# Window attention and SiLU MLP on one core: the second MLP product in float16 parts one group earlier, with w_out's two float32 parts joined on GpSimd

## The chip, the cores and the metric

One core of a Trainium2 chip. The metric is the device time of one execution in microseconds (us), the median of several runs. TensorE (PE) multiplies, VectorE (DVE), ScalarE (ACT) and GpSimd (POOL) work on tiles of 128 partitions, and SyncE (SP) issues most transfers. Each engine takes its own instructions in order and waits on semaphores for the others.

## The reference

```python
scores = scale * q @ k.T            # 8 batches x 8 heads x 576 rows, head size 64
scores = where((rel >= 0) & (rel < 128), scores + slope[h] * -abs(rel), -1e9)
x = softmax(scores) @ v             # joined to 4608 tokens x 512
h = x @ w_in                        # 512 x 2048
out = (h * sigmoid(h)) @ w_out      # 2048 x 512
```

All inputs and the output are float32.

## The kernel before

The 4608 tokens are taken in 9 groups of 512. A group g has 16 blocks f of 128 columns of the hidden layer, and the block n = 16 g + f is the unit of the MLP: `gemm1(n)` (L710) makes the 128 x 512 block of h, `act1` takes the tanh on ACT (L753), `act2` on DVE makes the activation from it and from h in PSUM (L762), `act3` writes its high part gh (L779), `act4` the rest gl (L796), and `gemm2(n)` (L917) adds gh and gl times w_out's block to four PSUM banks, with twelve matmuls of 128 x 512: (gh, high), (gh, low), (gl, high) for each of four token tiles.

Float32 accuracy comes from products of parts. In the early groups the parts are in the reduced float32 format fp32r: each weight block is held as a high and a low fp32r tile (`w_parts`, L983; the tags `w0_f` for w_in and `w1_f` for w_out). In later groups they are in float16, scaled by a power of two that a maximum over the weights gives. `IN16 = 2` and `OUT16 = 3` (L57) are the first groups whose first and second product use float16 parts. In groups below `OUT16`, act3 is a copy to fp32r and act4 runs on POOL (on DVE in the blocks at a group's edge, L807); from `OUT16` on, act3 is an ACT activation and act4 a `scalar_tensor_tensor` on DVE (L805).

The float16 weights are made in the middle of the kernel from the fp32r parts:

- `w_stat` (L237), 32 ACT activations, gives sums of squares; `wscale_finish` (L314) reduces them with a transpose, small DVE operations and a matmul to the two scales.
- For each of the 16 blocks of each matrix, `conv1` (L1009, ACT) writes the float16 high part, `conv2` (L1020, DVE) the remainder of the high part in float32, and `conv3` (L1028, DVE) adds the low part to it: three instructions, two of them on DVE.

The order of the work is written out by hand. The program runs through numbered steps; a step is half a `gemm1` or half a `gemm2`, so that a group is 64 steps: group 1 is steps 64 to 127, group 2 is 128 to 191. `put(step, function, ...)` files further work, which is issued ahead of the step's matmuls, by rank within a step (L1168: `normalize` first, then the activations, then `row_max` and `p_lo`, then all else). A step number fixes only where an instruction stands in its engine's queue; when it runs is decided by its waits.

The attention runs as such further work, one pair p (half a token tile's heads) in 8 steps: `scores` at step n (PE), `row_max` n + 1 (DVE), `exps` n + 2 and n + 3, `p_hi` (ACT) and `p_lo` (DVE) n + 3 to n + 5, a DMA transpose, `attend` n + 13 in the groups spoken of here (n + 12 from the third batch pair on), `normalize` (DVE) one step behind that. In group 2 the scores stand at steps 130, 138, 146, 154 and so on. PSUM's two banks with the tag `a` serve both the scores and the `attend` results, so `scores` of a pair must wait until `normalize`, two steps earlier, has read the bank. Every second pair, `load_v` (SP) fetches a tile rv, and `v_hi` (POOL, L427) and `v_lo` (DVE, L433) split it. In group 2 DVE also takes maxima of v for the next batches (`vscale_reduce`, L210).

In the kernel before, `STATS = 66` puts one `w_stat` in each step from 66 on, `CONV_IN = 106` starts w_in's conversions (four steps for each block, and three steps later from block 5 on: `CLEAR = 3`), and `CONV_OUT = 172` starts w_out's.

Of the kernel before, what the change touches and what calls it, by code (L numbers as in the profile page):

```python
# [6 lines left out]
F32 = mybir.dt.float32  # L7
# [26 lines left out]
NF = DFF // P  # L34
# [19 lines left out]
SLICE = 4  # L54


IN16, OUT16 = 2, 3  # L57
QK16 = 2
STATS16 = ("w1_10", "w1_11")
OWN = ("w1_12", "w1_13")  # L60
# [9 lines left out]
SUMS, SUMS_STEP = 332, 14  # L70
SUM_TAGS = tuple(f"w1_{k}" for k in range(7, 15))
MORE_TAGS = (("w1_15", 1), ("k", KSLOTS), ("k", KSLOTS))
STATS, CONV_IN, CONV_OUT = 66, 106, 172
CLEAR = 3
STEP = 8
LEAD = 14
XD = GT
# [20 lines left out]
def tile_window_attention_then_silu_mlp(ctx, tc, qk, qk16, v, w_in, w_out, distance, out):  # L98
    nc = tc.nc

    const = ctx.enter_context(tc.tile_pool(name="const", bufs=1))
    pool = ctx.enter_context(tc.tile_pool(name="pool", bufs=2))
    psum = ctx.enter_context(tc.tile_pool(name="psum", bufs=1, space=PSUM))

    ident = const.tile([P, P], F32, name="ident")
    tab = const.tile([P, H, 2 * P], BF16, name="tab")
    ones = const.tile([P, P], F32, name="ones")
# [32 lines left out]
    def f32(ap):  # L140
        return ap.bitcast(F32)
# [33 lines left out]
    vred = {}  # L175
# [59 lines left out]
    wsc = {}  # L235

    def w_stat(which, f):  # L237

        if f == 0:
            vred["w", which] = {"m": pool.tile([P, NF], F32, tag=f"stat{which}", bufs=1, name=f"stat{which}")}  # L240
        junk = pool.tile([P, DM], BF16, tag="xs", bufs=2, name=f"wj{which}_{f}")
        nc.scalar.activation(
            junk, f32(w_parts(f, which)[0]), AF.Square, accum_out=vred["w", which]["m"][:, f : f + 1]
        )
# [66 lines left out]
        flat = tab.rearrange("p h c -> p (h c)")  # L311
        nc.vector.tensor_scalar_mul(flat, flat, ratio)

    def wscale_finish(stage):  # L314

        if stage == 0:
            vred["w", "col"] = col = pool.tile([P, 3], F32, tag="vcol", name="vcolw")
            for k in range(2):
                nc.vector.tensor_reduce(col[:, k : k + 1], vred["w", k]["m"], axis=AX.X, op=ALU.max)
        elif stage == 1:  # L320
            ps = ps_of(next_tag("misc"), "vtw")
            for k in range(2):
                nc.tensor.transpose(ps[:1, k * P : (k + 1) * P], vred["w", "col"][:, k : k + 1], ident)
            vred["w", "row"] = row = pool.tile([P, 9], F32, tag="row", bufs=1, name="roww")
            c, inv = row[:1, 0:2], row[:1, 2:4]
            ci = c.bitcast(I32)
            nc.vector.tensor_reduce(c, ps[:1, : 2 * P].rearrange("p (k i) -> p k i", k=2), axis=AX.X, op=ALU.max)
            nc.vector.tensor_single_scalar(ci, ci, 0x7F800000, op=ALU.bitwise_and)
            nc.vector.tensor_single_scalar(ci, ci, 1, op=ALU.logical_shift_right)
            nc.vector.tensor_single_scalar(ci, ci, 0x1FC00000, op=ALU.add)  # L330
            nc.vector.tensor_single_scalar(ci, ci, 0x7F800000, op=ALU.bitwise_and)
            nc.vector.tensor_single_scalar(ci[:, 1:2], ci[:, 1:2], 1 << 23, op=ALU.add)
            nc.vector.tensor_single_scalar(inv.bitcast(I32), ci, -(14 << 23), op=ALU.add)
            nc.vector.tensor_scalar(ci, ci, -1, 268 << 23, op0=ALU.mult, op1=ALU.add)
        else:
            ps = ps_of(next_tag("misc"), "vsw")
            nc.tensor.matmul(ps[:, 0:4], ones[:1, :], vred["w", "row"][:1, 0:4], start=True, stop=True)
            t = pool.tile([P, 4], F32, tag="wsc", bufs=1, name="vscw")
            nc.vector.tensor_copy(t, ps[:, 0:4])
            for k in range(2):  # L340
                wsc["w", k] = t.rearrange("p (s k) -> p k s", k=2)[:, k]
# [641 lines left out]
    def w_parts(f, which):  # L983
        if which == 0:
            return [weight(kind, f).rearrange("p a b -> p (a b)") for kind in ("wih", "wil")]
        return weight("woh", f), weight("wol", f)
# [7 lines left out]
        minus(nc.gpsimd, lo, wraw.pop((f, which))[1], f32(hi))  # L994


    w16, rest = {}, {}

    def w16_tile(which, f):

        j, k = divmod(f, 2)
        if ("pair", which, j) not in w16:
            tag = f"w0_{NF // 2 + j if which else j}"
            w16["pair", which, j] = pool.tile([P, 2, 2, DM], F16, tag=tag, bufs=1, name=f"w16_{which}_{j}")
        t = w16["pair", which, j][:, k]
        w16[which, f] = t if which else t.rearrange("p a (c f) -> p a c f", c=NCC)
        return t

    def conv1(which, f):  # L1009
        hi = w_parts(f, which)[0]  # L1010
        if which or f:
            t = w16_tile(which, f)
            parts = [t[:, k] for k in range(2)]
        else:
            parts = [pool.tile([P, DM], F16, tag="xs", bufs=2, name=f"wi16_{k}_{f}") for k in range(2)]
        rest[which, f] = parts
        out16 = parts[0]
        nc.scalar.activation(out16, f32(hi), AF.Copy, scale=wsc["w", which][:, 0:1])

    def conv2(which, f):  # L1020
        hi, out16 = w_parts(f, which)[0], rest[which, f][0]
        r = pool.tile([P, DM], F32, tag="io", name=f"wr16_{which}_{f}")
        rest[which, f].append(r)
        nc.vector.scalar_tensor_tensor(
            out=r, in0=f32(hi), scalar=wsc["w", which][:, 0:1], in1=out16, op0=ALU.mult, op1=ALU.subtract
        )

    def conv3(which, f):  # L1028
        out16, low16, r = rest.pop((which, f))
        nc.vector.scalar_tensor_tensor(  # L1030
            out=low16, in0=f32(w_parts(f, which)[1]), scalar=wsc["w", which][:, 0:1], in1=r, op0=ALU.mult, op1=ALU.add
        )
        if not which and not f:

            t = w16_tile(0, 0)
            for k, part in enumerate((out16, low16)):
                nc.scalar.copy(t[:, k], part)
# [8 lines left out]
    def put(point, fn, *a):  # L1046
        plan.setdefault(max(point, at(0)), []).append((fn, a))

    for p in range(NPAIR):
        i, q = divmod(p, 2)  # L1050
        n = at(p)
# [48 lines left out]
        if q == 0:  # L1100
# [74 lines left out]
    with tc.manual_schedule():  # L1175
# [41 lines left out]
        for g in range(NG):  # L1217
# [3 lines left out]
            for f in range(NF):  # L1221
                n = g * NF + f
# [5 lines left out]
                while len(waiting) > left:  # L1228
                    k = waiting.pop(0)
# [70 lines left out]
```

## Time and profile before

| | |
|---|---|
| runs | 923.24, 923.34, 923.34 us; median 923.34 |
| the profiled execution | 923.45 us, of which its span (first to last instruction) is 921.7 |
| PE busy | 910.2 us (99%) |
| DVE busy | 697.8 us (76%) |
| ACT busy | 579.0 us (63%) |
| POOL busy | 204.2 us (22%) |
| mean granted TensorE clock | 0.999 |

All times of the trace are in us from the span's start. Group 2's matmuls run from 256.57 to about 362. PE is busy nearly all the time, so that the kernel's time is PE's own work plus the few places where PE waits; what the other engines do costs time only where PE, in its order, comes to an instruction whose operand is not there yet.

### The profile page before, as it was taken

How to read it: one execution, taken by the hardware profiler on the slowest of the kernel's cores; microseconds unless marked ns; L12 is line 12 of the kernel's file. 1: busy time of each engine (PE TensorE's matmuls, PEld its weight loads, DVE VectorE, ACT ScalarE, POOL GpSimd, SP SyncE). 2: the span in 40 equal slices, each digit the busy share in tenths (PEclk: the TensorE clock that was granted, in tenths of full speed). 3: DMA queues.
4: the chain of work that ended last, by engine and by line, in shares of the span. 5: the costliest groups of instructions: out<-in, count | busy, mean ns of one | idle time of the engine just before them, and what ended most of it. 6: DMA issues, size and time to landing. Idle time of an engine off the chain costs nothing.

```text
span 921.7 us, 17985 instructions
## 1 busy us (share of the span) xinstructions
PE 910.2 (99%) x6765; PEld 604.6 (66%) x6765; DVE 697.8 (76%) x1703; ACT 579.0 (63%) x1195; POOL 204.2 (22%) x195
## 2 busy tenths in 40 slices
PE   9999999999999999999999999999999999999998
PEld 7867777777787887555555555555555555557887
DVE  6889876446777778898778879888888876645675
ACT  7778887685556764666677756666766665533332
POOL 2343442222221221000000003455655300000000
PEclk9999999999999999999999999999999999999999
DMA  8977825243376655434698746444554454311000
GB/s 314 393 181 221 258 58 138 69 92 69 81 208 159 172 127 127 104 102 102 126 246 217 204 104 160 115 104 103 160 109 109 102 166 104 89 35 59 1 24 23
DMA packets 198182, 122.94 MB, mean 133 GB/s; under 512 B 166480, under 2 KB 167632, under 8 KB 198096
## 3 DMA queue, kind: packets, MB, share of 16 engines
q1 hardware_dynamic: 197664, 121.41, 50.2%
q8 instruction: 53, 0.87, 0.4%
q10 hardware_dynamic: 432, 0.39, 0.1%
q14 instruction: 33, 0.27, 0.1%
HBM read 71.96 MB, written 9.44 MB: 88 GB/s over the span
## 4 chain that ended last, share of the span: by engine, by line
PE 83%; DVE 6%; ACT 2%; issue 1%; DVEq 0%; ACTq 0%
PE o L933 33%; PE h L733 24%; PE h L738 8%; PE av L555 4%; PE h L705 4%; PE m L840 3%; PE sp L451 3%; PE sp L458 2%; DVE hr L505 1%; DVE gt L764 1%; DVE t L481 0%; ACT t L491 0%; DVE w L1030 0%; DVE vmx L210 0%; DVE x L148 0%
## 5 line engine op out<-in xcount | busy, mean ns | idle before, releaser
L933 PE MATMUL o<-w,gh 128*128 128x512 f16 (+1 forms) x1024 | 313.3, 387 | 0.3 <-ACT gh L791 0.3
L733 PE MATMUL h<-xt,w 128*128 128x512 f16 (+1 forms) x1344 | 266.7, 349 | 0.0
L933 PE MATMUL o<-w,gl 128*128 128x512 f16 (+1 forms) x512 | 197.3, 385 | 0.3 <-DVE gl L148 0.2
L733 PEld LDWEIGHTS <-w 128*128 128x128 f16 x1344 | 125.8, 98 | 103.1 <-issue 2.2
L760 ACT ACTIVATE gt<-h,gsc 128x512 f32<-128x512 f32 x112 | 76.8, 686 | 183.5 <-PE h L733 164.3
L764 DVE SCALAR_TENSOR_TENSOR gt<-gt,h 128x512 f32<-128x512 f32 x144 | 98.3, 683 | 87.7 <-ACT gt L760 87.0
L491 ACT ACTIVATE t<-t,mx 128x256 f32<-128x256 f32 (+1 forms) x288 | 125.8, 486 | 5.7 <-DVE mx L481 5.5
L505 DVE SCALAR_TENSOR_TENSOR hr<-t,hr 128x512 f16<-128x512 f32 (+1 forms) x128 | 96.7, 761 | 30.7 <-ACT hr L500 30.6
L933 PEld LDWEIGHTS <-gh 128*128 128x128 f16 x640 | 62.2, 98 | 74.2 <-ACT gh L793 0.3
L738 PE MATMUL h<-xh,w 128*128 128x512 f32 x256 | 89.8, 405 | 0.0
L427 POOL TENSOR_SCALAR v<-rv,vsc 128x512 f16<-128x512 f32 x30 | 28.0, 933 | 277.1 <-DMA rv<-v 177.5
L805 DVE SCALAR_TENSOR_TENSOR gl<-gt,gh 128x512 f16<-128x512 f32 x80 | 61.9, 774 | 33.8 <-ACT gh L793 32.7
L933 PEld LDWEIGHTS o<-w,gh 128*128 128x128 f32 x384 | 69.8, 188 | 15.9 <-ACT gh L791 0.8
L146 POOL TENSOR_TENSOR gl<-gt,gh 128x512 fp32r<-128x512 f32 x30 | 38.5, 1284 | 164.2 <-ACT gh L791 148.9
L500 ACT ACTIVATE hr<-t 128x512 f16<-128x512 f32 (+1 forms) x128 | 71.7, 595 | 2.0 <-DVE vmx L210 2.0
L793 ACT ACTIVATE gh<-gt 128x512 f16<-128x512 f32 x80 | 50.3, 629 | 26.0 <-DVE gt L764 23.3
L555 PEld LDWEIGHTS <-hl 128*128 128x128 f16 x1464 | 51.4, 98 | 16.5 <-issue 5.2
L481 DVE CUSTOM_DVE_ANT_0 t<-sp,tab,vsc 128x256 f32<-128x256 f32 (+1 forms) x144 | 58.4, 460 | 1.1 <-PE sp L451 0.7
L933 PEld LDWEIGHTS <-gl 128*128 128x128 f16 x320 | 31.3, 98 | 38.6 <-DVE gl L805 1.0
L146 POOL TENSOR_TENSOR w<-wm,w 128x512 fp32r<-128x512 f32 x32 | 43.4, 1355 | 59.3 <-ACT w L990 59.0
L555 PE MATMUL av<-v,hl 128*128 128x65 f16 (+1 forms) x1464 | 54.8, 193 | 1.6 <-DVE mx L481 1.6
L738 PEld LDWEIGHTS h<-xh,w 128*128 128x128 f32 x256 | 48.1, 188 | 12.3 <-issue 0.2
(183 smaller groups left out, 1357.2 us busy)
## 6 DMA issues: line engine op xcount, KB each, us to landing
r<-qk SPq DMA_DIRECT2D x36, 512.0 KB, 4.1
qs<-qk SPq DMA_DIRECT2D x18, 512.0 KB, 5.2
wr<-w_in SPq DMA_DIRECT2D x16, 512.0 KB, 6.6
wr<-w_out SPq DMA_DIRECT2D x16, 512.0 KB, 6.3
out<-ot SPq DMA_DIRECT2D x32, 256.0 KB, 2.5
rv<-v SPq DMA_DIRECT2D x30, 256.0 KB, 4.0
vm<-v SPq DMA_DIRECT2D x27, 256.0 KB, 5.6
q<-qk SPq DMA_DIRECT2D x18, 256.0 KB, 3.6
```

What stands on the lines that cost most here:

```text
L146: engine.tensor_sub(out, a, b)
L481: nc.vector.tensor_tensor_reduce(out=st[p]["t"][u][:, h, 2 * P - n :], in0=st[p]["sp"][h][:, u, o].rearrange("p o c -> p (o c)"), in1=tab[ ...
L491: nc.scalar.activation(x, x, AF.Exp, bias=st[p]["mx"][:, 2 * u + h : 2 * u + h + 1], scale=-1.0)
L500: nc.scalar.activation(split_of(p, u, hr)[:, 0], t[:, :, 2 * P - n :], AF.Copy, scale=PSCALE)
L505: nc.vector.scalar_tensor_tensor(out=hr[:, 1], in0=t[:, :, 2 * P - n :], scalar=PSCALE, in1=hr[:, 0], op0=ALU.mult, op1=ALU.subtract)
L555: nc.tensor.matmul(av[:, 2 * u + h, : rhs.shape[-1]], lhs, rhs, start=(n == 0), stop=(n == len(seq) - 1), skip_group_check=True,)
L733: nc.tensor.matmul(o, w[:, wp, cc], x, start=start and k == 0, stop=stop, skip_group_check=True)
L738: nc.tensor.matmul(hps[n], w[:, cc], x, start=(half == 0 and i == 0), stop=(half == 1 and i == len(seq) - 1), skip_group_check=True,)
L760: nc.scalar.activation(gt, hps[n], AF.Tanh, scale=scale)
L764: nc.vector.scalar_tensor_tensor(out=gt, in0=gt, scalar=1.0, in1=hps[n], op0=ALU.add, op1=ALU.mult)
L805: nc.vector.scalar_tensor_tensor(out=gl, in0=gt, scalar=CUT, in1=gh, op0=ALU.mult, op1=ALU.subtract)
L933: nc.tensor.matmul(ops[ti], a[:, t], w, start=(f == 0 and i == 0), stop=(f == NF - 1 and i == len(seq) - 1), skip_group_check=True,)
```

## The change

`OUT16` becomes 2: group 2's second product, 192 matmuls, uses float16 parts, and with it act3 and act4 of group 2 take the form of the later groups (ACT and DVE instead of ACT and POOL).

So w_out must be converted earlier. Its statistics and scale are split from w_in's (`wscale_finish` runs once for each matrix), and the statistics of w_in are put closer together, from step 64, those of w_out from 82. w_in's conversions begin at step 83 (the last six blocks, f = 10 to 15, stand at 127 to 149) and w_out's at 118 (f = 0 and 1 at 118 to 123, f = 2 to 15 at 130 to 183). A new POOL instruction, `join_out`, adds w_out's high and low fp32r part back into one float32 tile, filed six steps ahead of the block's conversion, into the memory of the block before (the first into an `io` buffer). The conversion of a w_out block is then one ACT and one DVE instruction instead of one and two.

```diff
-IN16, OUT16 = 2, 3
+IN16, OUT16 = 2, 2
-STATS, CONV_IN, CONV_OUT = 66, 106, 172
-CLEAR = 3
+STATS = (64, 82)
+CONV = (83, 118)
+JOIN, CLEAR = 6, (9, 1)
...
+    def join_out(f):
+        hi, lo = (f32(part) for part in w_parts(f, 1))
+        if f:
+            t = pool.tile([P, 2, DM], F32, tag=f"w1_{f - 1}", bufs=1, name=f"wo{f}")[:, 0]
+        else:
+            t = pool.tile([P, DM], F32, tag="io", name="wo0")
+        joined[f] = t
+        nc.gpsimd.tensor_add(t, hi, lo)
...
     def conv1(which, f):
-        hi = w_parts(f, which)[0]
+        hi = joined[f] if which else f32(w_parts(f, 0)[0])
...
     def conv2(which, f):
-        hi, out16 = w_parts(f, which)[0], rest[which, f][0]
-        r = pool.tile([P, DM], F32, tag="io", name=f"wr16_{which}_{f}")
-        rest[which, f].append(r)
+        hi, (out16, low16) = joined.pop(f) if which else f32(w_parts(f, 0)[0]), rest[which, f]
+        out = low16 if which else pool.tile([P, DM], F32, tag="io", name=f"wr16_{f}")
+        rest[which, f].append(out)
...
     def conv3(which, f):
         out16, low16, r = rest.pop((which, f))
+        if which:
+            return
...
-    for k in range(2 * NF):
-        put(STATS + k, w_stat, k % 2, k // 2)
+    for f in range(NF):
+        put(STATS[0] + 2 * f // 3, w_stat, 0, f)
+        put(STATS[1] + f, w_stat, 1, f)
...
-    for which, n in enumerate((CONV_IN, CONV_OUT)):
+    for which in range(2):
         for f in range(NF):
+            n = CONV[which] + SLICE * f + (SLICE if f > CLEAR[which] else 0)
+            if which:
+                put(n - JOIN, join_out, f)
             for k, fn in enumerate((conv1, conv2, conv3)):
-                put(n + SLICE * f + (CLEAR if f > 4 else 0) + (k if which or f else 0), fn, which, f)
+                put(n + (k if which or f else 0), fn, which, f)
```

POOL's queue about the border of groups 1 and 2, before (gl is act4, v is `v_hi`; the number behind a name is the buffer's):

```order
L146 TENSOR_TENSOR gl_3042<-gt_3029,gh_3041 128x512
L146 TENSOR_TENSOR gl_3120<-gt_3104,gh_3119 128x512
L427 TENSOR_SCALAR v_67<-rv_3019,vsc_1955 128x8x64
L146 TENSOR_TENSOR gl_3326<-gt_3293,gh_3325 128x512
L146 TENSOR_TENSOR gl_3370<-gt_3354,gh_3369 128x512
L146 TENSOR_TENSOR gl_3467<-gt_3451,gh_3466 128x512
L427 TENSOR_SCALAR v_67<-rv_3337,vsc_1955 128x8x64
```

The same place now (wo is the joined tile, w_2 to w_9 the parts of w_out's blocks):

```order
L147 TENSOR_TENSOR gl_3084<-gt_3068,gh_3083 128x512
L147 TENSOR_TENSOR gl_3165<-gt_3148,gh_3164 128x512
L426 TENSOR_SCALAR v_67<-rv_3058,vsc_1955 128x8x64
L1015 TENSOR_TENSOR wo_3225<-w_2_830 128x512
L1015 TENSOR_TENSOR wo_3314<-w_3_939 128x512
L1015 TENSOR_TENSOR wo_3413<-w_4_1023 128x512
L1015 TENSOR_TENSOR wo_3517<-w_5_1131 128x512
L426 TENSOR_SCALAR v_67<-rv_3388,vsc_1955 128x8x64
L1015 TENSOR_TENSOR wo_3607<-w_6_1234 128x512
L1015 TENSOR_TENSOR wo_3706<-w_7_1316 128x512
L1015 TENSOR_TENSOR wo_3790<-w_8_1422 128x512
L1015 TENSOR_TENSOR wo_3885<-w_9_1522 128x512
```

Group 2's act4, each of which waited for ACT, is gone from POOL, and the joins, which wait only for POOL itself, stand in runs of four between two `v_hi`.

DVE's queue in the first steps of group 2, before (L764 is act2, L505 `p_lo`, L1024 and L1030 are conv2 and conv3, L573 to L582 `normalize`):

```order
L1030 SCALAR_TENSOR_TENSOR w_0_2_3143<-w_5_982,vscw,wr_0_5_3310 128x512
L210 TENSOR_REDUCE vmx_3340<-vm_0_3246 128x1
L764 SCALAR_TENSOR_TENSOR gt_3354<-gt_3354,h_3312 128x512
L505 SCALAR_TENSOR_TENSOR hr_0_3375<-t_0_3331,hr_0_3375 128x512
L1024 SCALAR_TENSOR_TENSOR wr_0_6_3393<-w_6_1088,vscw,w_0_3_3377 128x512
L505 SCALAR_TENSOR_TENSOR hr_1_3391<-t_1_3333,hr_1_3391 128x512
L1030 SCALAR_TENSOR_TENSOR w_0_3_3377<-w_6_1088,vscw,wr_0_6_3393 128x512
L573 TENSOR_SCALAR r_3453<-av_3413 128x4
L574 RECIPROCAL r_3453<-r_3453 128x4
L582 TENSOR_TENSOR xs_3456<-av_3413,r_3453 128x256
```

The same place now (L804 is act4; L1031 is conv2 and L1039 conv3, of w_in where they read w_11 and of w_out where they read wo):

```order
L1031 SCALAR_TENSOR_TENSOR w_1_1_3361<-wo_3225,vscw_2876,w_1_1_3361 128x512
L211 TENSOR_REDUCE vmx_3392<-vm_0_3293 128x1
L763 SCALAR_TENSOR_TENSOR gt_3406<-gt_3406,h_3363 128x512
L1031 SCALAR_TENSOR_TENSOR wr_11_3411<-w_11_1564,vscw_2415,w_0_5_3291 128x512
L804 SCALAR_TENSOR_TENSOR gl_3426<-gt_3406,gh_3425 128x512
L1039 SCALAR_TENSOR_TENSOR w_0_5_3291<-w_11_1564,vscw_2415,wr_11_3411 128x512
L504 SCALAR_TENSOR_TENSOR hr_0_3431<-t_0_3382,hr_0_3431 128x512
L504 SCALAR_TENSOR_TENSOR hr_1_3446<-t_1_3384,hr_1_3446 128x512
L1031 SCALAR_TENSOR_TENSOR w_1_1_3361<-wo_3314,vscw_2876,w_1_1_3361 128x512
L572 TENSOR_SCALAR r_3509<-av_3467 128x4
L573 RECIPROCAL r_3509<-r_3509 128x4
L581 TENSOR_TENSOR xs_3512<-av_3467,r_3509 128x256
```

Between act2 and `p_lo` stand three more instructions (act4 and w_in's conv2 and conv3), between `p_lo` and `normalize` one fewer.

More of the change, by code (lines that the diff above doesn't have):

```diff
@@ L239, in w_stat @@
         if f == 0:
-            vred["w", which] = {"m": pool.tile([P, NF], F32, tag=f"stat{which}", bufs=1, name=f"stat{which}")}
+            vred["w", which] = {"m": pool.tile([P, NF], F32, tag="stat", bufs=2, name=f"stat{which}")}
         junk = pool.tile([P, DM], BF16, tag="xs", bufs=2, name=f"wj{which}_{f}")
@@ L312, in rescale_bias, with wscale_finish @@
         nc.vector.tensor_scalar_mul(flat, flat, ratio)
-    def wscale_finish(stage):
+    def wscale_finish(which, stage):
+        r = vred["w", which]
         if stage == 0:
-            vred["w", "col"] = col = pool.tile([P, 3], F32, tag="vcol", name="vcolw")
-            for k in range(2):
-                nc.vector.tensor_reduce(col[:, k : k + 1], vred["w", k]["m"], axis=AX.X, op=ALU.max)
+            r["col"] = col = pool.tile([P, 3], F32, tag="vcol", name=f"vcolw{which}")
+            nc.vector.tensor_reduce(col[:, 0:1], r["m"], axis=AX.X, op=ALU.max)
         elif stage == 1:
[L321 to L325, printed above, removed]
+            ps = ps_of(next_tag("misc"), f"vtw{which}")
+            nc.tensor.transpose(ps[:1, :P], r["col"][:, 0:1], ident)
+            c, inv = r["col"][:1, 1:2], r["col"][:1, 2:3]
             ci = c.bitcast(I32)
-            nc.vector.tensor_reduce(c, ps[:1, : 2 * P].rearrange("p (k i) -> p k i", k=2), axis=AX.X, op=ALU.max)
+            nc.vector.tensor_reduce(c, ps[:1, :P], axis=AX.X, op=ALU.max)
             nc.vector.tensor_single_scalar(ci, ci, 0x7F800000, op=ALU.bitwise_and)
@@ L331, in wscale_finish @@
             nc.vector.tensor_single_scalar(ci, ci, 0x7F800000, op=ALU.bitwise_and)
-            nc.vector.tensor_single_scalar(ci[:, 1:2], ci[:, 1:2], 1 << 23, op=ALU.add)
+            if which:
+                nc.vector.tensor_single_scalar(ci, ci, 1 << 23, op=ALU.add)
             nc.vector.tensor_single_scalar(inv.bitcast(I32), ci, -(14 << 23), op=ALU.add)
@@ L335, in wscale_finish @@
         else:
[L336 to L341, printed above, removed]
+            ps = ps_of(next_tag("misc"), f"vsw{which}")
+            nc.tensor.matmul(ps[:, 0:2], ones[:1, :], r["col"][:1, 1:3], start=True, stop=True)
+            t = pool.tile([P, 2], F32, tag="wsc", bufs=2, name=f"vscw{which}")
+            nc.vector.tensor_copy(t, ps[:, 0:2])
+            wsc["w", which] = t
     unit, gsc = {}, {}
@@ L994, in w_lo @@
         minus(nc.gpsimd, lo, wraw.pop((f, which))[1], f32(hi))
-    w16, rest = {}, {}
+    w16, rest, joined = {}, {}, {}
     def w16_tile(which, f):
@@ L1016, in conv1 @@
         rest[which, f] = parts
-        out16 = parts[0]
-        nc.scalar.activation(out16, f32(hi), AF.Copy, scale=wsc["w", which][:, 0:1])
+        nc.scalar.activation(parts[0], hi, AF.Copy, scale=wsc["w", which][:, 0:1])
     def conv2(which, f):
-        hi, out16 = w_parts(f, which)[0], rest[which, f][0]
-        r = pool.tile([P, DM], F32, tag="io", name=f"wr16_{which}_{f}")
-        rest[which, f].append(r)
+        hi, (out16, low16) = joined.pop(f) if which else f32(w_parts(f, 0)[0]), rest[which, f]
+        out = low16 if which else pool.tile([P, DM], F32, tag="io", name=f"wr16_{f}")
+        rest[which, f].append(out)
         nc.vector.scalar_tensor_tensor(
-            out=r, in0=f32(hi), scalar=wsc["w", which][:, 0:1], in1=out16, op0=ALU.mult, op1=ALU.subtract
+            out=out, in0=hi, scalar=wsc["w", which][:, 0:1], in1=out16, op0=ALU.mult, op1=ALU.subtract
         )
@@ L1029, in conv3 @@
         out16, low16, r = rest.pop((which, f))
+        if which:
+            return
         nc.vector.scalar_tensor_tensor(
-            out=low16, in0=f32(w_parts(f, which)[1]), scalar=wsc["w", which][:, 0:1], in1=r, op0=ALU.mult, op1=ALU.add
+            out=low16, in0=f32(w_parts(f, 0)[1]), scalar=wsc["w", 0][:, 0:1], in1=r, op0=ALU.mult, op1=ALU.add
         )
[L1033 to L1037, printed above, removed]
+        if f:
+            return
+        t = w16_tile(0, 0)
+        for k, part in enumerate((out16, low16)):
+            nc.scalar.copy(t[:, k], part)
     SUM_WORK = (
@@ L1120, in tile_window_attention_then_silu_mlp @@
     for x, wait in enumerate((0, 2, 5)):
-        put(STATS + 2 * NF + 2 + wait, wscale_finish, x)
-    for which, n in enumerate((CONV_IN, CONV_OUT)):
+        put(STATS[0] + 12 + wait, wscale_finish, 0, x)
+        put(STATS[1] + NF + 2 + wait, wscale_finish, 1, x)
+    for which in range(2):
         for f in range(NF):
+            n = CONV[which] + SLICE * f + (SLICE if f > CLEAR[which] else 0)
+            if which:
+                put(n - JOIN, join_out, f)
             for k, fn in enumerate((conv1, conv2, conv3)):
-                put(n + SLICE * f + (CLEAR if f > 4 else 0) + (k if which or f else 0), fn, which, f)
+                put(n + (k if which or f else 0), fn, which, f)
     for g in range(1, NG):
```

## The prediction

> **What bounds the kernel now.** I read the page first. TensorE is busy all the time, and the chain that ended last runs mostly through it:
>
> ```profile
> PE 910.2 (99%) x6765; PEld 604.6 (66%) x6765; DVE 697.8 (76%) x1703; ACT 579.0 (63%) x1195; POOL 204.2 (22%) x195
> PE 83%; DVE 6%; ACT 2%; issue 1%; DVEq 0%; ACTq 0%
> ```
>
> So a change pays through shorter work on PE or through a wait of PE that goes, and costs through a new wait. Next, PE's own waits: group 2 has one of size, in which the scores of step 154 wait for a late `normalize` (L582) to free their bank.
>
> ```profile
> PE sp L458 <- DVE xs L582: 1.1, 1, 1.1
> ```
>
> Then the chain in order of time (start, length, what) for one pair of attention with two blocks of the MLP. First group 2, where the second product (L933) is in fp32r, then group 3, where it is in float16:
>
> ```profile
> 309.31 2.77 PE o L933 x12
> 312.08 1.36 PE sp L458 x16
> ...
> 322.28 2.77 PE o L933 x12
> 325.04 1.09 PE sp L458 x16
> 326.13 2.73 PE h L733 x24
> ...
> 331.62 1.33 PE h L733 x12
> 332.95 0.73 PE av L555 x24
> 333.68 1.31 PE h L733 x12
> 334.99 2.95 PE o L933 x12
> ```
>
> ```profile
> 365.85 2.70 PE h L733 x12
> 368.55 2.59 PE o L933 x12
> 371.13 1.29 PE h L733 x6
> 372.43 0.72 PE av L555 x24
> 373.15 1.29 PE h L733 x6
> ...
> 380.82 2.59 PE o L933 x12
> ```
>
> A pair takes 334.99 - 322.28 = 12.71 us in group 2 without a wait, and 12.97 where the scores take 1.36 instead of 1.09; in group 3 it takes 380.82 - 368.55 = 12.27.
>
> Last, how full VectorE is in the first three pairs of group 2 (the columns: stretch, its length, busy PE, PEld, DVE, ACT, POOL):
>
> ```profile
> 269.10:281.90 12.80, 12.80 (x116) 10.59 (x113) 10.20 (x25) 8.54 (x21) 3.39 (x3) 1.00 0.63 167
> 281.90:294.80 12.90, 12.90 (x115) 10.73 (x113) 9.12 (x25) 8.42 (x19) 2.55 (x2) 1.00 0.66 184
> 294.80:309.10 14.30, 13.22 (x116) 10.92 (x113) 10.19 (x26) 8.90 (x21) 3.39 (x3) 1.00 0.70 166
> ```
>
> **The float16 product.** Group 2's first product stays in 256-column moves, which cost 0.03 + 0.06 more for each pair than group 3's rows (2.73 against 2.70, 1.33 + 1.31 against 1.29 + 1.29). A pair of group 2 will therefore take 12.27 + 0.09 = 12.36. Eight pairs save between 8 x (12.71 - 12.36) = 2.8 and 8 x (12.97 - 12.36) = 4.9 us. I take 3.3, near the clean pair, because the extra in the other lies in its scores. The old wait of 1.1 goes with the queue that made it, unless a new one takes its place.
>
> **The second scale.** One matmul pair more stands in PE's queue; the nearest row is the scale of the next batches:
>
> ```profile
> 349.80 0.31 PE vs L299 x2
> ```
>
> That is +0.3 us (at most 0.5 with format changes); the transposes are as many as before. The small DVE operations fall at steps 76 to 81, the closer statistics on ACT at 64 to 74, both where those engines have gaps: cost nothing, a few tenths if not.
>
> Up to here: 923.45 (the profiled execution, span 921.7 and 1.75 around it) - 3.3 - 1.1 + 0.3 = **919.35**.
>
> **VectorE in the first three pairs of group 2.** Each pair now has six conversion instructions there instead of four (two blocks of w_in with two, two of w_out with one) and two act4 that POOL did before. From one start to the next these take 0.66 and 0.61:
>
> ```profile
> 269.90 0.75 DVE L1030 SCALAR_TENSOR_TENSOR w<-w,vscw,wr 128x512 f16<-128x512 f32 x1
> 270.56 0.16 DVE L573 TENSOR_SCALAR r<-av 128x4 f32<-128x4 f32 x1
> ...
> 274.19 1.17 DVE L1024 SCALAR_TENSOR_TENSOR wr<-w,vscw,w 128x512 f32<-128x512 f32 x1
> ...
> 574.52 0.69 DVE L805 SCALAR_TENSOR_TENSOR gl<-gt,gh 128x512 f16<-128x512 f32 x1
> 575.13 0.74 DVE L400 SCALAR_TENSOR_TENSOR k<-r,vsc,k 128x512 f16<-128x512 f32 x1
> ```
>
> So a pair gains 2 x 0.66 + 2 x 0.61 = 2.5 us. On 10.20, 9.12 and 10.19, less some 0.7 in the first and third that is waiting for POOL (0.4 in the row at 274.19, which takes 1.17 for 0.75, and 0.3 in the L148 ahead of it; next part), this makes 12.0, 11.6 and 12.0, against 12.36 of PE: full, with 0.4 us to spare for each pair. From step 150 on, w_in's share (four instructions a pair) is gone, and there is room again.
>
> **What VectorE shares with POOL.** Rows of the timeline show DVE instructions with two operands in SBUF stretched where they meet a POOL instruction:
>
> ```profile
> 245.59 1.28 POOL L146 TENSOR_TENSOR gl<-gt,gh 128x512 fp32r<-128x512 f32 x1 [5.11 <-ACT gh L791]
> 246.84 0.87 POOL L427 TENSOR_SCALAR v<-rv,vsc 128x512 f16<-128x512 f32 x1
> ```
>
> ```profile
> 245.85 1.30 DVE L148 SCALAR_TENSOR_TENSOR x<-xs,x 128x256 f16<-128x256 f32 x1 [0.33 <-ACT x L592]
> ...
> 328.22 0.42 DVE L148 SCALAR_TENSOR_TENSOR x<-xs,x 128x256 f16<-128x256 f32 x1 [2.83 <-ACT x L592]
> ```
>
> L148 takes 0.42 alone, but 1.30 behind POOL's gl, and ends 0.28 after it (247.15 against 246.87): DVE was held until POOL was through. A join has gl's shape, so 1.28 is its price, and DVE pays it whenever its next instruction has two operands in SBUF (conversions, act4, `p_lo`); act2 and `row_max`, which read PSUM, run beside it. [...]
>
> The joins are filed six steps ahead, but nothing holds POOL to the steps: they wait for POOL alone, so that a run of four starts as soon as the `v_hi` ahead of it is through, 4 x 1.28 = 5.1 us without a gap. That is the core of my forecast, at three places.
>
> *At the border.* The run wo2 to wo5 follows the `v_hi` of 246.84 and lasts from 247.7 to 252.8 or longer. In it falls the last block of group 1, whose gl PE waits for:
>
> ```profile
> 252.23 0.69 DVE L148 SCALAR_TENSOR_TENSOR gl<-gt,gh 128x512 fp32r<-128x512 f32 x1
> ```
>
> ```profile
> 253.42 0.40 PE L933 MATMUL o<-w,gl 128*128 128x512 f32 x1
> ```
>
> gl ended at 252.92 and was needed at 253.42: 0.5 to spare. If the run ends beside it, nothing is lost; if copy and gl each wait for a join, 2 x 1.28 - 0.5 = 2.1. I take 1.0.
>
> *The first pair of group 2.* The next run follows a `v_hi` that waits for its transfer:
>
> ```profile
> 260.23 0.54 SPq L419 DMA_DIRECT2D rv<-v  x1
> ...
> 286.12 0.46 SPq L419 DMA_DIRECT2D rv<-v  x1
> ```
>
> ```profile
> rv<-v SPq DMA_DIRECT2D x30, 256.0 KB, 4.0
> ```
>
> 260.23 + 4.0 + 0.87 = 265.1: the joins wo6 to wo9 run from there. DVE is then at the act2 behind the reduction, and its next six instructions all have two operands in SBUF. One join lies beside act2, three hold DVE for 3 x 1.28 = 3.8. What can be spared is what `normalize` had in hand in this place:
>
> ```profile
> 270.97 0.42 DVE L582 TENSOR_TENSOR xs<-av,r 128x256 f32<-128x256 f32 x1
> ```
>
> ```profile
> 272.08 1.16 PE L458 MATMUL sp<-k,q 64*128 64x128 f32 x16
> ```
>
> 272.08 - 271.39 = 0.7. PE waits 3.1 at the scores of step 138, with all of its queue behind.
>
> *The third pair.* The next `v_hi` follows the transfer of 286.12 (290.1, and about 4 later with what was lost); wo10 to wo13 meet the same stretch of DVE's queue. 3.8, less 0.4 to spare from each of two pairs: 3.0. The last two joins fall where DVE has room.
>
> New waits: 1.0 + 3.1 + 3.0 = 7.1, with ends at 0 (every join beside an instruction that reads PSUM) and 2.1 + 2 x (4 x 1.28 - 0.7) = 10.9 (every join of the two runs paid in full). 919.35 + 7.1 = 926.45; the median lay 0.1 below the profiled execution, so 926.4.
>
> **The rivals.**
>
> *The cover holds; faster.* For it: later in the kernel POOL runs as many instructions in one piece, DVE is held there too, `normalize` comes 14.43 us after the one before, and PE has no wait at all in that stage:
>
> ```profile
> 576.86 0.42 DVE L582 TENSOR_TENSOR xs<-av,r 128x256 f32<-128x256 f32 x1
> ...
> 591.29 0.42 DVE L582 TENSOR_TENSOR xs<-av,r 128x256 f32<-128x256 f32 x1
> ```
>
> Against it: there `attend` stands a step earlier before the scores that need its bank, and w_in's conversions are long done. If it holds, the sum is 919.35 and the time 919.3. It decides as long as DVE's lateness at `normalize` stays under the 0.7: 0.30.
>
> *One run bites; no change.* If the third pair's transfer comes late, its joins fall behind step 150, where DVE has room: 919.35 + 1.0 + 3.1 = 923.45, about 923.4. For it: that `v_hi` hangs on SP's queue, which stands behind DVE's own late `p_lo` (its transposes): 0.19.
>
> [...] Then DVE pays a fourth join in each run, the upper end: 919.35 + 10.9 = 930.2: 0.05.
>
> **How the numbers follow.** My forecast has 0.46 and gives 926.4; its own range is 924.9 to 929.8 (new waits of 5.6 to 10.5, border and runs between their ends). About 0.2% (1.85 us) is what a measurement of this kernel can tell from no change. Faster is the first rival, 0.30; same the second, 0.19; slower the forecast and the third rival, 0.51. For 8 in 10 the range must take in most of the first rival: its low end, 919.2, is 919.35 less 0.15 and leaves out its part in which the product saves more; 929.8 leaves out the third rival. Both signs hold chances, so the forecast's own range above says more than the whole one.
>
> **What would show it.** Right: in the changed profile group 2's L933 pieces of twelve take 2.59; POOL's joins stand in runs of four without gaps behind a `v_hi`; DVE instructions of two SBUF operands beside them take 1.2 to 1.9 us; PE waits for L581 at the scores of steps 138 and 154, some 3 us each, and about 1 us for the last gl of group 1. [...]

## The result, and the profile after

The changed kernel takes 928.93 us (median of 4 runs, 928.75 to 929.37); the kernel before took 923.29 beside it (923.09 to 923.34). The ratio is 1.0062, with a 95% interval of 1.0045 to 1.008: slower, by 5.6 us. The profiled execution is the one of 929.37, with a span of 927.6.

The page of the changed kernel: TensorE's busy time hardly fell, VectorE's and GpSimd's rose, and the chain that ended last runs less through PE and more through DVE.

```profile
PE 909.8 (98%) x6767; PEld 590.2 (64%) x6767; DVE 712.3 (77%) x1709; ACT 579.2 (62%) x1196; POOL 211.7 (23%) x196
PE 78%; DVE 9%; issue 2%; ACT 2%; POOL 0%; DVEq 0%; ACTq 0%; POOLq 0%
```

The float16 product is there. In the chain of the changed kernel, in group 2, a second product of twelve takes 2.59, where it took 2.77:

```profile
310.27 2.59 PE o L932 x12
```

PE's waits from 150 to 400 us (in total, how many, the longest). Before there was one, of 1.1:

```profile
PE sp L457 <- DVE xs L581: 5.8, 3, 3.7
PE o L932 <- DVE gl L149: 0.9, 1, 0.9
PE sp L457 <- DVE vsc L302: 0.4, 1, 0.4
```

The three at the scores, from the timeline of PE (in brackets the idle time ahead of the row, and what ended it). They are the scores of steps 138, 154 and 170:

```profile
278.19 2.04 PE L457 MATMUL sp<-k,q 64*128 64x128 f32 x14 [3.75 <-DVE xs L581]
...
306.42 1.13 PE L457 MATMUL sp<-k,q 64*128 64x128 f32 x14 [1.63 <-DVE xs L581]
...
332.00 1.13 PE L457 MATMUL sp<-k,q 64*128 64x128 f32 x14 [0.45 <-DVE xs L581]
```

What GpSimd did then: at the border of groups 1 and 2 and in the first pair of group 2 four joins (L1015) run in a row, each time behind a `v_hi` (L426). A join has the shape of gl, which took 1.28 where GpSimd was not held. In these runs it took 6.13 / 4 = 1.53 and 6.79 / 4 = 1.70:

```profile
247.54 1.39 POOL L426 TENSOR_SCALAR v<-rv,vsc 128x512 f16<-128x512 f32 x1
248.90 6.13 POOL L1015 TENSOR_TENSOR wo<-w 128x512 f32<-128x512 f32 x4
...
268.70 1.29 POOL L426 TENSOR_SCALAR v<-rv,vsc 128x512 f16<-128x512 f32 x1 [13.67 <-DMA rv<-v]
269.96 6.79 POOL L1015 TENSOR_TENSOR wo<-w 128x512 f32<-128x512 f32 x4
```

VectorE beside the first and the second run. In these rows each instruction with two operands in SBUF takes 1.65 to 1.8 instead of 0.7, and even the copy L790, with one, takes 0.82, where it takes 0.43 in the run without joins:

```profile
250.66 1.78 DVE L1031 SCALAR_TENSOR_TENSOR w<-wo,vscw,w 128x512 f16<-128x512 f32 x1
252.36 0.67 DVE L763 SCALAR_TENSOR_TENSOR gt<-gt,h 128x512 f32<-128x512 f32 x1
253.07 0.82 DVE L790 CAST gh<-gt 128x512 fp32r<-128x512 f32 x1
253.92 1.65 DVE L149 SCALAR_TENSOR_TENSOR gl<-gt,gh 128x512 fp32r<-128x512 f32 x1
```

```profile
270.45 1.79 DVE L1039 SCALAR_TENSOR_TENSOR w<-w,vscw,wr 128x512 f16<-128x512 f32 x1
272.17 3.47 DVE L504 SCALAR_TENSOR_TENSOR hr<-t,hr 128x512 f16<-128x512 f32 x2
275.55 1.75 DVE L1031 SCALAR_TENSOR_TENSOR w<-wo,vscw,w 128x512 f16<-128x512 f32 x1
...
277.62 0.42 DVE L581 TENSOR_TENSOR xs<-av,r 128x256 f32<-128x256 f32 x1
```

act2 (L763), which reads one of its two operands from PSUM, keeps its 0.67, and `row_max` (L480), which does the same, took 0.41 beside the first join (249.06), where it takes 0.414 in the run without joins. `normalize` (L581) comes at 277.62, and PE goes on at 278.19.

One thing in the windows is new in this stage (length, busy PE, PEld, DVE, ACT, POOL, then the granted clock of PE): at the end of the longest wait the clock falls to half.

```profile
276.00:278.00 2.00, 0.00 (x0) 0.00 (x0) 1.93 (x5) 0.00 (x0) 0.75 (x1) 0.98 0.70 156
278.00:280.00 2.00, 1.81 (x14) 1.77 (x14) 2.00 (x5) 1.33 (x3) 0.00 (x0) 0.50 0.00 0
280.00:282.00 2.00, 2.00 (x14) 1.46 (x13) 1.89 (x5) 2.00 (x6) 0.00 (x0) 0.67 0.47 116
282.00:284.00 2.00, 2.00 (x18) 1.50 (x17) 2.00 (x10) 0.52 (x2) 0.00 (x0) 1.00 1.07 322
```

In windows of 0.1 us the half clock lasts from 277.9 to 281.3, 3.4 us. In it the fourteen matmuls of the scores took 2.04, where they took 1.13 at 306.42.

Where the time went, by PE's own instructions (from each start to the next one, summed over the stretch between the first second product of one group and that of the next; the last column is the first experiment below):

| us | before | after | without joins |
|---|---|---|---|
| group 1, whole stretch | 105.19 | 107.84 | 106.22 |
| of it the second product | 45.46 | 47.71 | 46.09 |
| group 2, whole stretch | 105.45 | 108.96 | 102.13 |
| of it the second product | 46.95 | 42.24 | 42.24 |
| of it the first product | 40.98 | 42.60 | 42.05 |
| of it the scores, with the waits ahead of them | 11.07 | 17.70 | 11.41 |

Groups 3 to 7 agree within 0.02. The span's 5.9 are 2.65 in group 1, 3.51 in group 2, and -0.24 before them.

### The profile page after: what moved, and what is told of

It reads as the page before. It is cut to its first block, busy times and chain, and to the rows that moved or that the text cites. A ratio compares the mean times of both kernels' runs of the same rounds, so it can differ in the third digit from the quotient of the medians.

```text
span 927.6 us, 17962 instructions
## 1 busy us (share of the span) xinstructions
PE 909.8 (98%) x6767; PEld 590.2 (64%) x6767; DVE 712.3 (77%) x1709; ACT 579.2 (62%) x1196; POOL 211.7 (23%) x196
## 4 chain that ended last, share of the span: by engine, by line
PE 78%; DVE 9%; issue 2%; ACT 2%; POOL 0%; DVEq 0%; ACTq 0%; POOLq 0%
PE o L932 30%; PE h L732 24%; PE h L737 7%; PE h L704 4%; PE av L554 4%; PE m L839 3%; PE sp L450 3%; PE sp L457 2%; DVE hr L504 2%; DVE gt L763 1%; DVE w L1031 1%; DVE t L480 1%; ACT gh L792 1%; ACT t L490 1%; DVE gl L804 1%
## 5 line engine op out<-in xcount | busy, mean ns | idle before, releaser
L932 PE MATMUL o<-w,gh 128*128 128x512 f16 (+1 forms) x1024 | 310.1, 384 | 0.1
L763 DVE SCALAR_TENSOR_TENSOR gt<-gt,h 128x512 f32<-128x512 f32 x144 | 98.5, 684 | 93.7 <-ACT gt L759 93.4
L932 PEld LDWEIGHTS <-gh 128*128 128x128 f16 x768 | 74.6, 98 | 85.6 <-ACT gh L792 0.3
L504 DVE SCALAR_TENSOR_TENSOR hr<-t,hr 128x512 f16<-128x512 f32 (+1 forms) x128 | 103.5, 817 | 14.6 <-ACT hr L499 14.6
L426 POOL TENSOR_SCALAR v<-rv,vsc 128x512 f16<-128x512 f32 x30 | 28.3, 943 | 363.4 <-DMA rv<-v 241.3
L804 DVE SCALAR_TENSOR_TENSOR gl<-gt,gh 128x512 f16<-128x512 f32 x96 | 73.6, 766 | 45.9 <-ACT gh L792 44.6
L792 ACT ACTIVATE gh<-gt 128x512 f16<-128x512 f32 x96 | 60.4, 629 | 45.6 <-DVE gt L763 42.3
L932 PEld LDWEIGHTS <-gl 128*128 128x128 f16 x384 | 37.6, 98 | 46.3 <-DVE gl L804 1.4
L480 DVE CUSTOM_DVE_ANT_0 t<-sp,tab,vsc 128x256 f32<-128x256 f32 (+1 forms) x144 | 58.5, 461 | 1.5 <-PE sp L450 1.2
L932 PEld LDWEIGHTS o<-w,gh 128*128 128x128 f32 x256 | 46.8, 188 | 11.4 <-DVE gh L790 0.6
L480 DVE CUSTOM_DVE_ANT_0 t<-sp,tab 128x256 f32<-128x256 f32 (+1 forms) x144 | 50.1, 401 | 4.0 <-PE sp L457 3.8
```

Source lines behind the costliest of these rows:

```text
L480: nc.vector.tensor_tensor_reduce(out=st[p]["t"][u][:, h, 2 * P - n :], in0=st[p]["sp"][h][:, u, o].rearrange("p o c -> p (o c)"), in1=tab[ ...
L504: nc.vector.scalar_tensor_tensor(out=hr[:, 1], in0=t[:, :, 2 * P - n :], scalar=PSCALE, in1=hr[:, 0], op0=ALU.mult, op1=ALU.subtract)
L763: nc.vector.scalar_tensor_tensor(out=gt, in0=gt, scalar=1.0, in1=hps[n], op0=ALU.add, op1=ALU.mult)
L792: nc.scalar.activation(gh, gt, AF.Copy, scale=CUT)
L804: nc.vector.scalar_tensor_tensor(out=gl, in0=gt, scalar=CUT, in1=gh, op0=ALU.mult, op1=ALU.subtract)
L932: nc.tensor.matmul(ops[ti], a[:, t], w, start=(f == 0 and i == 0), stop=(f == NF - 1 and i == len(seq) - 1), skip_group_check=True,)
```

## The experiments

Theory, the "ports theory" of the expectations: beside joins, VectorE's instructions with two operands in SBUF come only in turn with them, as in the rows above (1.65 to 1.8 instead of 0.7), and VectorE, which by my estimate has 0.4 us to spare for each pair there, hands that on to PE. What the two engines share no run shows. Rivals: VectorE's own new work (conversions and act4) makes the waits; or the conversions wait for sums that come late.

### Joins left out

```diff
 def join_out(f):
     hi, lo = (f32(part) for part in w_parts(f, 1))
...
-    joined[f] = t
-    nc.gpsimd.tensor_add(t, hi, lo)
+    joined[f] = hi
```

> The changed kernel with the joins left out: the conversion of w_out reads the high part alone, so the low part of w_out is missing from the second product of groups 2 to 7. ScalarE's and VectorE's work stays as it is, GpSimd has nothing but v_hi in group 2. [...] Rival (VectorE is too full by the conversions and act4 alone): the waits stay, 926 or more.

Measured: 920.9 us, ratio to the kernel before 0.9977 (0.9968 to 0.9985), mean clock 0.999 to 1.0; 0.4 above the 919 to 920.5 that I gave for the theory. Its waits of PE from 150 to 400:

```profile
PE sp L457 <- DVE xs L581: 0.9, 2, 0.6
PE sp L457 <- DVE vsc L302: 0.4, 1, 0.4
```

And VectorE at the same place of the program as above, `p_lo`, conv2, `normalize`:

```profile
269.35 1.28 DVE L504 SCALAR_TENSOR_TENSOR hr<-t,hr 128x512 f16<-128x512 f32 x2
270.56 0.74 DVE L1026 SCALAR_TENSOR_TENSOR w<-w,vscw,w 128x512 f16<-128x512 f32 x1
...
271.61 0.42 DVE L581 TENSOR_TENSOR xs<-av,r 128x256 f32<-128x256 f32 x1
```

The same instructions take 1.28 and 0.74 instead of 3.47 and 1.75. So the joins cost 0.85% (1.0062 against 0.9977), 7.8 us, and without them the rest of the change is a gain of 2.1. VectorE's load alone leaves three small waits, 1.3 together.

### Every join made twice

```diff
-    nc.gpsimd.tensor_add(t, hi, lo)
+    for _ in range(2):
+        nc.gpsimd.tensor_add(t, hi, lo)
```

> Each join made twice by GpSimd (the same sum into the same place). Ports theory: each run holds VectorE for four more joins; the waits at 138 and 154 grow by 4 to 5 us each, both are then long enough to bring the half clock, 938 to 944. Rival (VectorE's load, not GpSimd): within 1 us of the changed kernel.

Measured: 936.19 us, 1.0142 (1.0126 to 1.0157): once more 7.4 us. That is 2 below the range that I gave: the wait at step 138 hardly grew (3.98), because `normalize` meets the same four joins; the further four hit the next pair (0.96), and the second run now brings 3.61 at step 154. From the timeline of GpSimd, and of PE:

```profile
269.56 13.22 POOL L1016 TENSOR_TENSOR wo<-w 128x512 f32<-128x512 f32 x8
```

```profile
277.85 2.04 PE L457 MATMUL sp<-k,q 64*128 64x128 f32 x14 [3.98 <-DVE xs L581]
293.21 1.13 PE L457 MATMUL sp<-k,q 64*128 64x128 f32 x14 [0.96 <-DVE xs L581]
309.61 2.04 PE L457 MATMUL sp<-k,q 64*128 64x128 f32 x14 [3.61 <-DVE xs L581]
```

The half clock came with both long waits, from 277.84 for 3.41 us and from 308.56 for 6.83.

### The sums made for nobody

```diff
-    joined[f] = t
-    nc.gpsimd.tensor_add(t, hi, lo)
+    joined[f] = hi
+    nc.gpsimd.tensor_add(w_parts(f, 1)[1], hi, lo)
```

> GpSimd makes the same 16 sums, filed at the same steps, but into the place of w_out's low part, which nothing reads later; the conversion reads the high part alone, as in the run without joins (so the low part is missing from the second product of groups 2 to 7). No instruction waits for a join. Ports theory: the waits of the changed kernel stay, with the half clock: 927 to 930. Rival (the conversions, and VectorE behind them, wait for sums that come late): as without joins, 920.5 to 921.5.

Measured: 929.66 us, 1.0071 (1.0059 to 1.0084), all the loss of the changed kernel. No conversion waits for these sums, so it is GpSimd's running that costs, not the data. Its timelines of GpSimd and of VectorE in the first pair:

```profile
270.33 6.72 POOL L1011 TENSOR_TENSOR w<-w 128x512 fp32r<-128x512 f32 x4
```

```profile
270.82 1.75 DVE L1035 SCALAR_TENSOR_TENSOR w<-w,vscw,wr 128x512 f16<-128x512 f32 x1
272.50 3.43 DVE L504 SCALAR_TENSOR_TENSOR hr<-t,hr 128x512 f16<-128x512 f32 x2
275.86 1.74 DVE L1027 SCALAR_TENSOR_TENSOR w<-w,vscw,w 128x512 f16<-128x512 f32 x1
```

Four joins and four VectorE instructions alternate: (1.75 + 3.43 + 1.74) / 4 = 1.73 for each, one join of 1.28 and a remainder of its own.

### Both parts by VectorE, nothing joined

```diff
-            if which:
-                put(n - JOIN, join_out, f)
...
-        hi = joined[f] if which else f32(w_parts(f, 0)[0])
+        hi = f32(w_parts(f, which)[0])
...
-        hi, (out16, low16) = joined.pop(f) if which else f32(w_parts(f, 0)[0]), rest[which, f]
-        out = low16 if which else pool.tile([P, DM], F32, tag="io", name=f"wr16_{f}")
+        hi, (out16, low16) = f32(w_parts(f, which)[0]), rest[which, f]
+        out = pool.tile([P, DM], F32, tag="io", name=f"wr16_{which}_{f}")
...
-        if which:
-            return
...
-            out=low16, in0=f32(w_parts(f, 0)[1]), scalar=wsc["w", 0][:, 0:1], in1=r, op0=ALU.mult, op1=ALU.add
+            out=low16, in0=f32(w_parts(f, which)[1]), scalar=wsc["w", which][:, 0:1], in1=r, op0=ALU.mult, op1=ALU.add
...
```

> The float16 product from group 2 on, with w_out converted from its two parts by two VectorE instructions as before the change, and nothing joined by GpSimd. VectorE gets 16 instructions of 0.66 more (10.6 us), two in each pair of attention. Ports theory: GpSimd is silent, and each of the first three pairs of group 2 is about 1 us too long on VectorE, 0.7 to spare: waits of some 2 to 3 us together, no half clock, 921 to 924. Rival (VectorE's load alone makes the waits): worse than the changed kernel, 930 or more.

Measured: 922.63 us, 0.9995 (0.9987 to 1.0004). Sixteen more instructions on VectorE cost 1.7 us over the run without joins; sixteen on GpSimd cost 7.8. PE's waits:

```profile
PE sp L457 <- DVE xs L581: 2.0, 2, 1.2
...
PE o L932 <- DVE gl L804: 0.3, 1, 0.3
```

### w_in's last blocks converted later

```diff
-            n = CONV[which] + SLICE * f + (SLICE if f > CLEAR[which] else 0)
+            n = CONV[which] + SLICE * f + (SLICE * (1 if which else f - CLEAR[0]) if f > CLEAR[which] else 0)
```

> The changed kernel with w_in's blocks 11 to 15 converted 8 steps apart instead of 4, so that each of the first three pairs of group 2 has one block (two VectorE instructions, 1.3 us) less and later pairs have it instead. The joins stay in runs of four. If a run costs what VectorE lacks to spare, the wait at step 138 falls from 3.7 to about 2.4, too short for the clock to fall, and that at 154 from 2.1 to under 1: 924 to 926. Rival (a run of four costs its length whatever else VectorE has to do): both waits stay, 928 to 929.

Measured: 926.63 us, 1.0041 (1.0029 to 1.0054), between the ranges that I gave for the two outcomes. The profile is of the longest run, 927.53. In it the wait at step 138 fell by 1.0, not 1.3, and that at 154 only from 1.63 to 1.48. So what VectorE has to spare sets part of the wait, the run's length the rest. And the half clock did not go: that 2.4 would be too short for it was an estimate of mine, between the 3.75 and the 1.63 of the changed kernel, and with 2.71 us of waiting it came, from 277.55 for 3.41 us. PE's row:

```profile
276.54 1.13 PE L457 MATMUL sp<-k,q 64*128 64x128 f32 x14 [2.71 <-DVE xs L581]
```

### attend a step earlier

```diff
-            a = n + (15 if p < 4 * GT else 13 if i < QK16 * NBLK else 12)
+            a = n + (15 if p < 4 * GT else 13 if n < 114 else 12)
```

> The changed kernel with attend, and normalize behind it, one step (about 1.5 us) earlier for the pairs of group 2, so that normalize has that much more in hand before the scores that need its bank. Joins and conversions as they are. If VectorE's lateness at normalize is the wait, the 3.7 us at step 138 fall to about 2.2 and the half clock behind them may go, those at 154 and later fall to nearly nothing; the border keeps its 1.6: 924 to 926. Rival (attend itself then waits, for p_lo's transposes behind the held VectorE): the wait moves to attend, 928 to 930.

The edit moves `v_hi` and `v_lo` of these pairs with attend; on GpSimd four joins still stand behind each `v_hi`.

Measured: 924.19 us, 1.0015 (1.0006 to 1.0024). The waits for `normalize` nearly go and the clock stays whole (mean 1.0); the rival was half right, since the lateness comes out at `attend` and at the second product instead, in small pieces:

```profile
PE av L554 <- DVE mx L480: 1.0, 1, 1.0
PE sp L457 <- DVE vsc L302: 0.8, 1, 0.8
PE o L932 <- DVE gh L790: 0.7, 1, 0.7
PE o L932 <- DVE gl L804: 0.6, 1, 0.6
...
PE sp L457 <- DVE xs L581: 0.4, 1, 0.4
```

### Joins held to a block each

```diff
+    last = [None]
...
         gact[n] = (gh, gl, gt)
+        last[0] = gh
...
+        beat = pool.tile([P, 1], F32, tag="beat", name=f"beat{f}")
+        nc.gpsimd.tensor_copy(beat, f32(last[0])[:, 0:1] if last[0].dtype == F32R else last[0][:, 0:1])
         nc.gpsimd.tensor_add(t, hi, lo)
```

> The changed kernel with a copy of one column of the latest block's gh ahead of each join on GpSimd, so that a join runs when ScalarE has made that gh, one in each block, not four in a row. If the sum of what VectorE loses counts, two joins in a pair cost it up to 2.6 us where 0.4 are spare: waits of 1 to 2 at each of the scores of steps 138, 146 and 154, none long enough for the half clock: 924 to 928. Rival (only the bunching costs): the waits of group 2 nearly go, 921 to 923.

Measured: 926.54 us, 1.0028 (1.0018 to 1.0039), in two groups of runs, 924.4 and 926.6; why there are two stays open, since the profile is of one of 924.45, and the mean clock is 0.998 in runs of both. In that profile the border costs nothing: group 1's stretch is 106.22, as without joins, because the joins now stand behind the last gh (released at 252.39) and `gl` takes its 0.69:

```profile
252.39 0.71 POOL L1018 COPY beat<-gh 128x1 f32<-128x1 f32 x1 [3.99 <-DVE gh L791]
253.06 1.29 POOL L1019 TENSOR_TENSOR wo<-w 128x512 f32<-128x512 f32 x1
```

```profile
251.90 0.43 DVE L791 CAST gh<-gt 128x512 fp32r<-128x512 f32 x1
252.36 0.69 DVE L149 SCALAR_TENSOR_TENSOR gl<-gt,gh 128x512 fp32r<-128x512 f32 x1
```

In group 2 the waits are 0.63, 1.55 and 0.20 (steps 138, 146 and 154). So bunching makes the longest wait, and the sum that VectorE loses still costs some. The half clock, which I had not expected behind waits of 1 to 2 (the changed kernel had none behind its 1.63), came after a wait of 1.55, from 288.05 for 3.41 us:

```profile
287.21 1.28 PE L457 MATMUL sp<-k,q 64*128 64x128 f32 x14 [1.55 <-DVE xs L581]
```

### Both parts by VectorE, and w_in's last blocks later

The edit of `dve_parts` with the line of `slow_win`.

> Both parts of w_out converted by VectorE, nothing joined, and w_in's blocks 11 to 15 converted 8 steps apart. VectorE has 1.3 us less in each of the first three pairs of group 2 than in the run without joins that converts both parts. If its load makes the waits that are left there (0.6 at a block's second product, 1.5 and 1.1 at scores), they go: 920.5 to 921.5. If they come of something else, 922.3 to 923.

Measured: 921.51 us, 0.9984 (0.9975 to 0.9993). PE's waits for `normalize` fell from 2.0 to 1.5 in all, a part of what I had expected:

```profile
PE sp L457 <- DVE xs L581: 1.5, 2, 0.8
```

### The same with attend a step earlier

The line of `attend_early` on top.

> As the kernel before it here (both parts on VectorE, w_in's last blocks 8 steps apart), with attend one step earlier for the pairs of group 2 as well. If what is left are waits for normalize, 919.5 to 920.5, 0.3% under the kernel before; if attend has to wait for its transposes instead, 921 to 923.

Measured: 920.38 us, 0.9972 (0.9961 to 0.9984): a version that beats both kernels. Its scores wait no more for `normalize`, but the wait for the next batch's scale grew from 0.4 to 1.2:

```profile
PE sp L457 <- DVE vsc L302: 1.2, 1, 1.2
```

### attend earlier only for steps 114 to 159

The edits of `dve_slow`, and this in place of the line of `attend_early`.

```diff
-            a = n + (15 if p < 4 * GT else 13 if i < QK16 * NBLK else 12)
+            a = n + (15 if p < 4 * GT else 13 if i < QK16 * NBLK and not 114 <= n < 160 else 12)
```

> Both parts of w_out on VectorE, nothing joined, w_in's last blocks 8 steps apart, attend one step earlier only for the pairs of steps 114 to 159 of group 2 (not for the one ahead of the next batch's scale, whose wait grew from 0.4 to 1.2 where all of group 2 had it). If that wait was the price of the earlier attend, 919.4 to 920.2; if it comes of VectorE's load, 920.3 to 921 as with all pairs.

Measured: 920.56 us, 0.9972 (0.9961 to 0.9983), no better. The scale's wait is back at 0.4 and a new one of 0.5 for `normalize` stands where the pairs change over. The time lies in the range that I had given for VectorE's load. So the wait moved with attend, but the total did not fall; that VectorE's load sets it is argued, not shown by a run of its own.

## Why the prediction was right, and where its sizes were off

The forecast had the right mechanism and direction: 926.4 against 928.9, 2.5 us too low. Step by step:

- **The float16 product**, forecast -3.3: the two products of group 2 together went from 46.95 + 40.98 = 87.93 to 42.24 + 42.05 = 84.29 in the run without joins, -3.6. Right.
- **The old wait of 1.1 goes**: wrong. It went with its queue, but VectorE's new load put three smaller waits in its place (0.6, 0.3 and 0.4 without joins), so that the scores took 11.41 after 11.07, where the sum had 1.1 less. I had worked out 0.4 us to spare for each pair and priced the lateness of a full VectorE at nothing.
- **The second scale**, forecast +0.3: measured 0.31 (the two scale pairs take 0.62 in group 1). That format changes could make it 0.5 no run shows: both pairs took the 0.31 of the row that I had gone by. The closer statistics on ScalarE, "a few tenths if not" hidden, cost 0.4: the first second product of group 1 took 3.21 instead of 2.80, because ScalarE came to the gh of that block 0.5 later (156.25 after 155.73), behind those statistics. So I had priced ScalarE too low. With the row above, and other small differences, the clean sum of 919.35 came out at 920.8 in the profiled execution without joins.
- **The border**, forecast 1.0 between 0 and 2.1: 47.71 - 46.09 = 1.6. 0.3 of it is PE's for a late gh and 1.3 for a late gl. The copy L790 did wait: it took 0.82 after 0.43 and ended 0.29 behind the join beside it (253.89 after 253.60). The measured 1.6 lies between the 1.0 that I took and the 2.1 for copy and gl both held.
- **The first pair**, forecast 3.1: the wait was 3.75. The run met four VectorE instructions, not three, for the `v_hi` came at 268.70 and not at 264: the transfer was issued 2.6 later than before, at 262.86, and landed 5.8 after its issue, where I had taken 4.0. From its L1039 to `normalize` VectorE took 277.62 - 270.45 = 7.17, and 2.92 without joins, so that it lost 4.25 where I had reckoned 3.8. The third rival had four joins paid in each run (4 x 1.28 - 0.7 = 4.4); 3.75 lies midway between that and my 3.1. But no two joins ran ahead of one such instruction here: the four joins took 6.79 and the four instructions beside them 1.79 + 3.47 + 1.75 = 7.01, one join to each.
- **The half clock behind it**: not in the sum at all. On PE's own rows it cost 1.5: 0.55 in the first product (42.60 against 42.05) and 0.9 in the scores, which took 2.04 for fourteen instead of 1.13. Whether the whole kernel pays that much stays open. With w_in's last blocks later, the one run with a mean clock of 1.0 took 926.47, and four at 0.998 took 926.58 to 927.53; with the joins held to a block, one at 1.0 took 924.42, and two at 0.998 took 924.44 and 924.45. Against that, the sums made for nobody took longest, 930.15 and 931.04, where the mean clock was lowest, 0.997 and 0.996. A slower PE also comes later to the next place where it would wait, which may give part of it back.
- **The third pair**, forecast 3.0: 1.63, and 0.45 two pairs later. The run of four was there (299.33, 6.72), but it began one VectorE instruction later: L1039 stood beside `v_hi` and the joins held three instructions. From L1039 to L581 VectorE took 305.84 - 298.81 = 7.03, and 4.27 without joins, so that it lost 2.76 and not 4.25:

```profile
298.81 1.10 DVE L1039 SCALAR_TENSOR_TENSOR w<-w,vscw,wr 128x512 f16<-128x512 f32 x1
...
305.84 0.42 DVE L581 TENSOR_TENSOR xs<-av,r 128x256 f32<-128x256 f32 x1
```

Of the 4.27, 0.65 is a wait of VectorE for ScalarE, which the joins hid. PE's wait grew from 0.28 without joins to 1.63, by 1.35 and not by 2.76. That VectorE had caught up by the rest, in PE's standstill and half clock before it, can only be argued.

The new waits, forecast 7.1 in all, measured 927.6 - 919.0 = 8.6 between the spans with and without joins: border 1.6, group 2 6.8. Without the 1.5 of the half clock that is the forecast's 7.1, but this agreement is luck: the border and the first pair cost more than I had reckoned, the third pair less. The first rival, that the cover holds, fell with the waits; the second, that one run alone bites, fell with the 1.63 at step 154.

## What to carry to other kernels

Before giving work to an idle engine, look for what its running does to the full one: here sixteen GpSimd sums cost 7.8 us, and sixteen more instructions on the busy VectorE in their place cost 1.7. A queue that nothing held back ran in bunches here as soon as it was released, four joins in 6.13 to 6.79 us, whatever step the work was filed at; price such a bunch against what the victim has in hand, at the place where the release lets it fall. And look for the granted clock behind a wait of TensorE: here it fell to half behind waits of 1.55 to 3.98 us, though not behind one of 1.63.

## What the hardware showed that I had not expected

After some waits PE was granted half its clock for 3.41 us (6.83 in one case). The wait was 3.75, 3.68, 2.71, 3.98, 3.61 and once only 1.55; waits of 1.63, 1.49, 1.48 and 1.33 did not bring it. So length alone does not decide.

In the changed kernel's trace the clock stands whole for 273.07 us, from its first entry at 4.84, at half for 3.41 and whole for 645.12, 80, 1 and 189 times 3.413. With every join made twice it is at half from 277.84 for 3.41, whole for 27.31, and at half from 308.56 for 6.83, 1, 8 and 2 times as much; 1.05 of the second wait lay behind that last fall. In the 3.41 us ahead of each fall in group 2 PE idled 3.41 in the changed kernel, 3.41 and 2.6 with every join made twice, 2.9 with the sums made for nobody, 2.4 with w_in's last blocks later and 1.55 with the joins held to a block. Cut into lengths of 3.413 from the first entry on, the traces of the two kernels hold two more falls, at their ends (919.69 before, 926.44 after), with 2.11 and 2.93 of idle ahead; in every other length at the whole clock PE idled 1.20 or less. The wait of 1.63 lies across the border of two such lengths, with 0.4 in one and 1.2 in the other. The two nearest cases, each with the length behind it (columns as above; the idle time is the length less PE's busy time), are the run with the joins held to a block and the one with w_in's last blocks later:

```profile
284.63:288.05 3.42, 1.87 (x18) 1.26 (x17) 3.35 (x8) 2.49 (x7) 0.00 (x0) 1.00 0.41 82
288.05:291.46 3.41, 3.41 (x19) 2.33 (x17) 3.32 (x5) 1.86 (x4) 2.45 (x2) 0.50 0.98 236
```

```profile
301.44:304.86 3.42, 1.94 (x11) 0.88 (x10) 3.35 (x7) 0.00 (x0) 1.31 (x1) 1.00 0.61 137
304.86:308.27 3.41, 3.41 (x37) 3.04 (x38) 3.35 (x10) 2.77 (x7) 0.00 (x0) 1.00 0.77 235
```

An idle time of 1.55 has the half clock behind it, one of 1.48 has not. That the idle time counted in this way decides is an estimate of mine from these cases.

GpSimd and VectorE took turns beside a run of joins: in the first pair four VectorE instructions with two operands in SBUF took 1.74 to 1.79 each, where they took 0.64 to 0.74 without joins, and the four joins 6.79 / 4 = 1.70 instead of 1.28, so that both lost.
